# First batch's queries and keys loaded in rows of four tokens and turned by plain products; first chunk's input products in three single-pass products; a new table of costs and due times

## Chip, cores, metric

One core of one Trainium2 chip runs the kernel. The metric is device time in microseconds (us) of one execution; the time before is the median of 3 runs.

## What is computed

Three blocks in a row, in float32. The inputs are q, k, v of 4 batches x 8 heads x 576 tokens x 64 and, as 64-bit floats, the weights of two feed-forward blocks.

```python
# attention, per batch and head
q_d, k_d, v_d = (t.reshape(B, H, 144, 4, D).mean(axis=3) for t in (q, k, v))
out = repeat(softmax(q_d k_d^T / 8) v_d, 4) + softmax(where(|i-j| < 4, q k^T / 8, -1e9)) v
x = out as 2304 tokens x 512
# first block: 512 -> 2048 -> 512
h = x @ w_in;  g = where(h > 0, h, exp(min(h, 0)) - 1);  x2 = g @ w_out
# second block: 512 -> 2 x 1536 -> 512
y = (silu(x2 @ w_gate) * (x2 @ w_val)) @ w_o2
```

## The kernel before

**Stages.** The 2304 tokens of the first block are 8 chunks of 288 (`T1`), each made of 3 units of 96 tokens (`U`); a batch is 6 units. Chunk 0 is units 0 to 2 of batch 0, chunk 1 its units 3 to 5, chunk 2 the first half of batch 1. The head of the program does batch 0's attention. Then come 8 x 16 steps (chunk c, slice f of 128 of the 2048 inner columns): `gemm1` (h = w_in[f] x), the ELU (L984 and L992 on ACT, L988 on DVE), a split of g into two words (copy L307 or L309, subtraction L995 on POOL), and `gemm2`, which adds into 4 PSUM banks that hold the chunk's result. The attention of batches 1 to 3 and the preparation of later weights are threaded between these steps. The second block follows; it multiplies 2x2 blocks of matrices with 7 products (`add_seven`).

**Two ways to multiply.** A plain float32 product takes several passes in TensorE. `products` (L911 to L917) writes each operand as the sum of two words of type float32r, high and low, and makes three single-pass products: high x high (L915), high x low (L916), low x high (L917). A weight is split by `add_weight_split`: a copy gives the high word, a subtraction on POOL (L451) the low one. Chunk 0 uses plain products for both gemms (`add_whole`, L940 and L945), so its weights and its x need no split; chunks 1 to 7 use the three products for both.

**Weights.** They arrive as 64-bit floats (`load_w`, L363 and L368, 512 KB each) and are turned into float32 by `add_weights`: two ACT instructions (L404, L407) and two DVE instructions (L411, L413) per slice and matrix, 32 in the first block.

**Batch 0's attention.** `add_unit` loads q (96 tokens) and k (112) of one unit, token by partition, in pieces of 256 B (`load_rows`, L494), turns them with TensorE transpositions (L633), copies the result out of PSUM (`keep`, by L307 on ACT) and sums groups of four tokens (`add_sums`: L519 on DVE or L524 and L525 on POOL). `add_local` does the 7-wide local attention of a unit: scores (L541), mask (L558), maxima (L563), subtraction (L566), exp (L569), sum and reciprocal (L572 to L574), weighting (L577), 32x32 transposition (L580), spreading into `bd` (L309 or L307), values (L606). `add_pooled` does the pooled attention of two heads p: sums of four v rows (`add_rows`, L696 on DVE or L700 and L701 on POOL), scores (L717), maxima (L724, L725), exps (L730), weighting (L740 on DVE), transposition (L758), values (L774), and a copy to `xdT`. `add_split` adds local and pooled parts. For chunk 0 it is one DVE instruction per unit (L893, x<-f,xdT). For later chunks it adds (L893, f<-f,xdT, DVE or POOL), copies the high word (ACT or DVE) and subtracts for the low word (L903 on POOL).

**Order.** Every instruction group is a task of `Work`: the engine or engines that may run it with a cost, a due time, what it reads and writes. `Work.run` plays the tasks in a model and emits them engine by engine, the earliest due ready task first. Costs and due times (`START`, `STEP0`, `STEP`, `EAGER`, `URGENT`, `FREE`, `SLACK`, `spans`, `w2_away` and numbers in each `add`) decide the order; on the chip every engine then runs its own list in that order. DMAs are issued by SP in list order.

Of the kernel before, what the change touches and what calls it, by code (L numbers as in the profile page):

```python
# [27 lines left out]
KU = 112  # L28
# [109 lines left out]
class Work:  # L138
# [6 lines left out]
    CHANGE = 0.1  # L145
# [114 lines left out]
def attention_moe_moe(ctx: ExitStack, tc: tile.TileContext, q, k, v, w_in, w_out, w_gate, w_val, w_o2, ident_in, mask_in, band_in, picks_in, out):  # L260
# [20 lines left out]
    U0, U1 = 2, 19  # L281
# [95 lines left out]
    def add_words(due, raw, u, reads=()):  # L377
# [14 lines left out]
        add("act", 0.42, due - 4.1, rest, reads=[raw, *reads], writes=[raw])  # L392
        add("act", 0.42, due - 4, size, reads=[raw, *reads], writes=[u])
        return add("dve", 1.0, due - 2.5, words, reads=[raw, u], writes=[u])

    def add_weights(keys, dues, whole):

        made = {}
        for n, key in enumerate(keys):
# [16 lines left out]
            add("sp", 0.5, due - 36.0, lambda key=key, raw=raw: load_w(key, raw.t), writes=[raw], nbytes=P * 4096)  # L416
            add("act", 0.69, due - 4, rest, reads=[raw, w.whole], writes=[w])
            add("act", 0.69, due - 3.5, size, reads=[raw], writes=[ps])
            made[key] = add("dve", 1.5, due - 2.5, words, reads=[raw, w, ps], writes=[w, ps])
# [25 lines left out]
    def add_weight_split(key, due, w, copiers=COPIER):  # L445

        wt[key] = w
        u = ww[key]
        add(copiers, (0.62, 0.9)[:len(copiers)], due - 2, lambda engine="act": copy(engine, w.t[:, 0], u.t.bitcast(F32)),
            reads=[u], writes=[w], second=0)  # L450
        return add("pool", 1.3, due - 1, lambda: nc.gpsimd.tensor_tensor(  # L451
            out=w.t[:, 1], in0=u.t.bitcast(F32), in1=w.t[:, 0], op=ALU.subtract), reads=[u, w], writes=[w])
# [19 lines left out]
    PAD, QW = R - 1, U + QB - SB  # L472
    KW, LONG = KU + 2 * PAD + 2, S + 8
    turned = {
        name: pools["att"].tile(shape, F32, tag=name, name=name)
        for name, shape in (("qT", [P, NP * LONG]), ("kT", [P, NP * LONG]), ("bd", [P, 2, H, U]), ("sm", [P, 2, H, QB]))}
    places, longs = {}, {}
    for name, w in (("qT", QW), ("kT", KW)):
        places[name] = Places(lambda i, t=turned[name], w=w: t[:, i * NP * w:(i + 1) * NP * w].rearrange("p (a t) -> p a t", a=NP), LONG // w)
        longs[name] = Places(lambda i, t=turned[name]: t[:, i * LONG:(i + 1) * LONG], NP)  # L480
    for name in ("bd", "sm"):
        places[name] = Places(lambda i, t=turned[name]: t[:, i:i + 1], 2)
    twos = {name: Both(places[name], turned[name]) for name in ("bd", "sm")}
# [28 lines left out]
    def add_sums(due, x, to, reads, writes, cost):  # L512
# [3 lines left out]
        def pool(engine):  # L516
# [10 lines left out]
        return add(EITHER, cost, due, pool, reads=reads, writes=[*writes, half])  # L527

    def add_local(i, n, due, q_of, k_of, reads, off, tvs, then=()):

        start = i * U if n > 1 else 0
        sc, pvs = [att_bank(), att_bank()], [att_bank() for _ in range(n)]

        def scores():
            for u in range(n):
                for p in range(NP):
                    for s in range(NB):
                        a = start + u * U + s * SB
                        first = off + a - (R - 1)
                        for j in range(2):  # L540
                            nc.tensor.matmul(  # L541
                                sc[j].t[s * QB:(s + 1) * QB, (u * NP + p) * QB:(u * NP + p + 1) * QB],
                                q_of(p)[j * D:(j + 1) * D, a:a + QB], k_of(p)[j * D:(j + 1) * D, first:first + QB],
                                start=True, stop=True)

        sm, bd = (twos[name].new() if n > 1 else place(name) for name in ("sm", "bd"))
# [5 lines left out]
        add("pe", 0.8 * n, due + 2 - EAGER, scores, reads=reads, writes=[*sc, sm], slack=SLACK, kind="small", after=then)  # L552
# [12 lines left out]
        def less(engine):  # L565
            two(engine).tensor_tensor(out=both(sm.t), in0=both(sm.t), in1=sums_of().to_broadcast([P, n * H, QB]), op=ALU.subtract)  # L566
# [9 lines left out]
        def weight(engine):  # L576
# [13 lines left out]
        add("dve", cost(0.56, 0.28), due + 3 - FREE, masked, reads=sc, writes=[sm])  # L590
# [939 lines left out]
```

## Time and profile before

| | us |
|---|---|
| median of 3 runs (lowest, highest) | 963.61 (963.43, 965.06) |
| the profiled execution | 962.43 |
| its span, first to last instruction | 960.6 |
| busy in the span: PE / DVE / ACT / POOL | 924.7 / 587.9 / 519.6 / 488.8 |
| mean granted TensorE clock | 0.982 of full |

Three stretches of the span matter here: the head, until the first `gemm1` begins; chunk 0, in which both gemms are plain; and chunks 1 to 7. "Busy" is the union of an engine's instructions; an instruction's own duration can overlap the next by some hundredths of a microsecond. A plain product is recorded as two PE instructions, a float32r product as one.

### The profile page before, as it was taken

To read this page: it belongs to the slowest core of one execution; us is meant where nothing else is said; L and a number is where in the kernel's file an instruction comes from. 1 tells how busy PE (TensorE), PEld (TensorE's weight loads), DVE (VectorE), ACT (ScalarE), POOL (GpSimd) and SP (SyncE) were. 2 spreads that over 40 slices of the span, in tenths; PEclk is the share of its full clock that TensorE was granted. 3 is DMA by queue.
4 is the path that set the end of the run, shared out by engine and by line. 5 is a ranking of instruction groups with operands and counts; after the bars stand their busy time and mean duration, and the time that the engine had idled before them with its cause. 6 is when DMAs were issued, how large, how long until landed. Compare 5 with 4: busy or idle time off the path is not lost.

```text
span 960.6 us, 20374 instructions
## 1 busy us (share of the span) xinstructions
PE 924.7 (96%) x7738; PEld 838.2 (87%) x7738; DVE 587.9 (61%) x1023; ACT 519.6 (54%) x1191; POOL 488.8 (51%) x554
## 2 busy tenths in 40 slices
PE   6799999999989999999899999999999999999998
PEld 4577788899979999999899988888888887899998
DVE  5999777988886687646115567222222225886773
ACT  3878864665744665656445564634333426444441
POOL 5322994564553433428932537998777939100000
PEclk8689999999999999999999999999999999999999
DMA  9899514945673444546432254440313269953331
GB/s 173 251 319 250 93 40 121 164 144 141 162 159 94 129 135 124 154 128 199 149 94 81 83 184 182 162 176 23 121 51 114 99 208 322 314 165 112 124 129 44
DMA packets 189730, 142.07 MB, mean 148 GB/s; under 512 B 101184, under 2 KB 170944, under 8 KB 189632
## 3 DMA queue, kind: packets, MB, share of 16 engines
q1 hardware_dynamic: 189488, 140.50, 50.0%
q8 instruction: 61, 1.00, 0.4%
q14 instruction: 37, 0.30, 0.1%
q10 hardware_dynamic: 144, 0.26, 0.1%
HBM read 96.68 MB, written 44.04 MB: 146 GB/s over the span
## 4 chain that ended last, share of the span: by engine, by line
PE 85%; DVE 5%; ACT 2%; POOL 2%; SPq 2%; DMA 2%; issue 2%; DVEq 0%; ACTq 0%; POOLq 0%
PE bank L915 25%; PE bank L917 24%; PE bank L916 24%; PE bank L940 4%; PE bank L945 3%; PE bank L606 1%; PE bank L541 1%; SPq L662 1%; PE bank L817 1%; PE bank L823 1%; PE warm L1416 0%; DVE e L988 0%; PE bank L870 0%; DMA kT<-in_k_dram 0%; DMA x2d<-o 0%
## 5 line engine op out<-in xcount | busy, mean ns | idle before, releaser
L995 POOL TENSOR_TENSOR g<-e,g 128x288 fp32r<-128x288 f32 x112 | 96.3, 861 | 150.3 <-ACT g L307 115.6
L915 PE MATMUL bank<-x,w 128*128 128x288 f32 x448 | 136.3, 304 | 10.0 <-DVE e L988 9.8
L915 PE MATMUL bank<-g,w 128*128 128x288 f32 x448 | 135.2, 302 | 0.0
L916 PE MATMUL bank<-x,w 128*128 128x288 f32 x448 | 132.9, 297 | 1.6 <-POOL x L903 1.6
L915 PE MATMUL bank<-xs,wu 128*128 128x512 f32 x336 | 132.6, 395 | 0.5 <-DVE blk L1119 0.5
L916 PE MATMUL bank<-g,w 128*128 128x288 f32 x448 | 132.1, 295 | 0.7 <-issue 0.7
L916 PE MATMUL bank<-xs,wu 128*128 128x512 f32 x336 | 132.6, 395 | 0.0
L917 PE MATMUL bank<-xs,wu 128*128 128x512 f32 x336 | 132.6, 394 | 0.0
L917 PE MATMUL bank<-x,w 128*128 128x288 f32 x448 | 132.4, 296 | 0.0
L917 PE MATMUL bank<-g,w 128*128 128x288 f32 x448 | 131.8, 294 | 0.0
L1119 DVE TENSOR_TENSOR blk<-bank,blk 128x512 f32<-128x512 f32 x72 | 49.7, 691 | 99.1 <-PE bank L917 90.7
L915 PE MATMUL bank<-os,ys 128*128 128x256 f32 x378 | 107.3, 284 | 1.5 <-DVE o L1119 1.0
L917 PE MATMUL bank<-os,ys 128*128 128x256 f32 x378 | 107.0, 283 | 0.4 <-DVE ys L1087 0.4
L916 PE MATMUL bank<-os,ys 128*128 128x256 f32 x378 | 106.9, 283 | 0.0
L988 DVE SCALAR_TENSOR_TENSOR e<-e,bank 128x288 f32<-128x288 f32 x112 | 50.1, 449 | 82.9 <-ACT e L992 76.9
L915 PEld LDWEIGHTS bank<-x,w 128*128 128x128 f32 x448 | 84.6, 189 | 14.4 <-DVE e L988 13.1
L1116 ACT COPY blk<-bank 128x512 f32<-128x512 f32 x72 | 42.2, 586 | 88.6 <-PE bank L917 87.2
L984 ACT ACTIVATE e<-bank 128x288 f32<-128x288 f32 x112 | 45.7, 410 | 80.4 <-PE bank L917 50.8
L916 PEld LDWEIGHTS bank<-x,w 128*128 128x128 f32 x448 | 85.2, 190 | 1.9 <-POOL x L903 1.8
L915 PEld LDWEIGHTS bank<-g,w 128*128 128x128 f32 x448 | 84.0, 187 | 3.2 <-issue 1.5
L917 PEld LDWEIGHTS bank<-g,w 128*128 128x128 f32 x448 | 84.5, 189 | 0.8 <-issue 0.8
L917 PEld LDWEIGHTS bank<-x,w 128*128 128x128 f32 x448 | 85.1, 190 | 0.0
(170 smaller groups left out, 2315.2 us busy)
## 6 DMA issues: line engine op xcount, KB each, us to landing
yr<-yd SPq DMA_DIRECT2D x27, 512.0 KB
yd<-blk SPq DMA_DIRECT2D x24, 512.0 KB
os<-od SPq DMA_DIRECT2D x42, 256.0 KB
u<-wd SPq DMA_DIRECT2D x40, 256.0 KB
wd<-mid SPq DMA_DIRECT2D x72, 128.0 KB
w<-in_moe_w_in_dram SPq DMA_DIRECT2D x16, 512.0 KB
w<-in_moe_w_out_dram SPq DMA_DIRECT2D x16, 512.0 KB
w<-in_moe_w_out_dram SPq DMA_DIRECT2D x24, 256.0 KB
```

Of the source, the lines that this page charges most:

```text
L541: nc.tensor.matmul(sc[j].t[s * QB:(s + 1) * QB, (u * NP + p) * QB:(u * NP + p + 1) * QB], q_of(p)[j * D:(j + 1) * D, a:a + QB], k_of(p)[j ...
L606: nc.tensor.matmul(pvs[u].t[j * D:(j + 1) * D, p * U:(p + 1) * U], tvs[u].t[:, (2 * p + j) * D:(2 * p + j + 1) * D], bd.t[:, u, j * NP + p ...
L915: nc.tensor.matmul(ps, sh, mh, start=first, stop=False, skip_group_check=more)
L916: nc.tensor.matmul(ps, sh, ml, start=False, stop=False, skip_group_check=more)
L917: nc.tensor.matmul(ps, sl, mh, start=False, stop=last, skip_group_check=more)
L940: nc.tensor.matmul(h.t[:, :T1], wi.t[:, i * P:(i + 1) * P].bitcast(F32), x.t[:, i, 0].bitcast(F32), start=i == 0, stop=i == NP - 1)
L945: nc.tensor.matmul(acc[0][i].t[:, :T1], wo.t[:, i * P:(i + 1) * P].bitcast(F32), ge(), start=f == 0, stop=f == NF1 - 1)
L984: nc.scalar.activation(e.t, h.t[:, :T1], AF.Relu, scale=-1.0)
L988: nc.vector.scalar_tensor_tensor(out=e.t, in0=e.t, scalar=-1.0, op0=ALU.add, in1=h.t[:, :T1], op1=ALU.max)
L995: add("pool", 0.82, due - URGENT, lambda e=e, g=g: nc.gpsimd.tensor_tensor(out=g.t[:, 1], in0=e.t, in1=g.t[:, 0], op=ALU.subtract), reads= ...
L1116: return add("act", ps_copy, when(m) - 20, lambda: nc.scalar.copy(d(i), ps.t[:, :w]), reads=[ps], writes=of(i))
L1119: return add("dve", ps_sum, when(m) - 20, lambda: nc.vector.tensor_tensor(out=d(i), in0=ps.t[:, :w], in1=d(i), op=ALU.add), reads=[ps], wr ...
```

## The change

1. Batch 0's q and k come in 16 DMAs (`add_first_batch`), each 72 rows x 2 heads x 4 tokens, in pieces of 1 KB, instead of 12. Each is turned by 8 plain products with the identity (64 x 72 each) instead of 4 transpositions per load; a copy takes 288 columns out of PSUM, and the sums of four are made per piece of 72. Sums of k may only go to POOL now, those of q to DVE or POOL.
2. Sums of four v rows in batch 0 go to POOL alone (`VS`), its pooled weighting to DVE or POOL.
3. `gemm1` of chunk 0 makes the three float32r products. So the 16 input weights are split before chunk 0's steps, the copy by POOL or ACT (POOL preferred), and x of chunk 0 is split into two words as in later chunks.
4. New costs, due times, 19 instead of 17 slots for whole weights, and new rows for `sm` of batch 0.

Pairs of input weights now share a slot, as do pairs of output weights. The counts of the second block's instructions stay.

```diff
-    START, STEP0, STEP, STEP2 = 48.0, 4.1, 3.45, 7.9
+    START, STEP0, STEP, STEP2 = 29.4, 3.73, 3.68, 7.9
-    EAGER, URGENT, FREE, SLACK = 15.0, 14.0, 8.0, 1.0
+    VS, VC = EITHER[1:], (1.25,)
+    FIRST, VALUES, LATER, POOLED, EARLY, PREFER = -40.0, -16.0, 117.2, 1.5, 2.8, -16.0
+    EAGER, URGENT, FREE, SLACK = 32.9, 20.2, 14.9, 0.0
...
+    def add_first_batch(rows, ready):
+
+        sums[0] = sum_ring.new()
+        parts = {name: [longs[name].new(lambda p=p: [p]) for p in range(NP)] for name in ("qT", "kT")}
+        made = {}
+        for k, (p, u, which) in enumerate((p, u, which) for p in range(NP) for u in range(2) for which in range(2)):
+            name, start = (("qT", 0), ("kT", PAD))[which]
+            t, dst, pt = rows[k], parts[name][p], att_bank()
+            cols = slice(start + u * UPC * U, start + (u + 1) * UPC * U)
+            add("sp", 0.5, FIRST + 0.5 * k, lambda t=t, p=p, u=u, name=name: nc.sync.dma_start(
+                out=t.t, in_=rows_of(name[0], 0, u, 2 * p, 2 * p + 2)), writes=[t], nbytes=HALF * 2048 * 1.2)
+
+            def turn(t=t, pt=pt):
+                for r in range(R):
+                    for j in range(2):
+                        nc.tensor.matmul(
+                            pt.t[j * D:(j + 1) * D, :UPC * U].rearrange("c (g r) -> c g r", r=R)[:, :, r],
+                            t.t[:, j, r * D:(r + 1) * D], ident[:HALF, :HALF], start=True, stop=True)
+
+            add("pe", 0.62, FIRST + k - EAGER, turn, reads=[t], writes=[pt, dst], slack=SLACK, kind="small", after=ready[:1])
+            made[which, p, u] = add(COPIER, (0.41, 0.45), FIRST + k + 1, lambda engine, dst=dst, pt=pt, cols=cols: copy(
+                engine, dst.t[:, cols], pt.t[:, :UPC * U]), reads=[pt], writes=[dst], second=1)
+            summed.setdefault((0, p), []).append(add_sums(
...
+                holds=[dst], after=[made[which, p, u]], engines=EITHER[which:]))
+        return parts, made
...
-            add(EITHER, (1.0, 1.25), due, lambda engine, u=u, t=t: add_rows(u, t.t, engine), reads=[t], writes=[vs])
+            add(VS, VC, due, lambda engine="pool", u=u, t=t: add_rows(u, t.t, engine), reads=[t], writes=[vs])
...
-        if c == 0:
-            return add("dve", 0.8, due, lambda: both("dve", x.t[:, :, 0, cols].bitcast(F32)), reads=[xf, xdT[b]], writes=[x])
...
-        wi, wo, x = ww["in", f], ww["out", f], xt[0]
+        add_weight_split(("in", f), due - EARLY, w_slots.new(lambda: range(NW)), ("pool", "act"), PREFER)
+        wi, wo, x = wt["in", f], ww["out", f], xt[0]
...
         def gemm1():
             begun.append(1)
             for i in range(NP):
-                nc.tensor.matmul(
-                    h.t[:, :T1], wi.t[:, i * P:(i + 1) * P].bitcast(F32), x.t[:, i, 0].bitcast(F32), start=i == 0, stop=i == NP - 1)
+                cs = slice(i * P, (i + 1) * P)
+                products(h.t[:, :T1], (wi.t[:, 0, cs], wi.t[:, 1, cs]), (x.t[:, i, 0], x.t[:, i, 1]), i == 0, i == NP - 1)
...
-            return time1(2 * NF1) + (time1(6.9 * NF1) - time1(2 * NF1)) * m / (2 * len(w2))
+            return time1(2.4 * NF1) + (time1(7.6 * NF1) - time1(2.4 * NF1)) * m / (2 * len(w2))
...
-        spans = {1: (18, 25), 2: (40, 50), 3: (70, 80)}
+        spans = {1: (14.8, 16.8), 2: (28.1, 79.7), 3: (66.3, 178.5)}
```

What moves, at three places. The names are tiles: `bank` a PSUM bank, `w` a slot that holds weights or, in the head, attention rows, `x` the chunk's input, `g` the ELU's output.

PE, end of the head, before:

```order
L758 MATMUL bank<-ident,w 72x72 x8
L541 MATMUL bank<-kT,qT 32x32 x32
L774 MATMUL bank<-prT,vs 64x144 x4
L606 MATMUL bank<-bd,w 64x96 x8
L940 MATMUL bank<-x,w 128x288 x8
L945 MATMUL bank<-g,w 128x288 x4
```

PE, end of the head, now:

```order
L605 MATMUL bank<-bd,w 64x96 x8
L748 MATMUL bank<-ident,w 72x72 x8
L764 MATMUL bank<-w,vs 64x144 x4
L605 MATMUL bank<-bd,w 64x96 x8
L538 MATMUL bank<-kT,qT 32x32 x32
L903 MATMUL bank<-x,w 128x288
L904 MATMUL bank<-x,w 128x288
L905 MATMUL bank<-x,w 128x288
```

The first slices of `gemm1` are single-pass products now; three slices of them (36 products) stand ahead of the first `gemm2`, where two slices (8 plain products) did.

POOL, at the end of the head, before:

```order
L577 TENSOR_TENSOR sm<-sm,st 128x256
L566 TENSOR_TENSOR sm<-sm,st 128x256
L451 TENSOR_TENSOR w<-w 128x512 x2
L893 TENSOR_TENSOR f<-f,xdT 128x384
L577 TENSOR_TENSOR sm<-sm,st 128x256
```

POOL, at the end of the head, now (the last row is the last one that the first `gemm1` waits for):

```order
L506 MEMSET w 32x512
L310 CAST w<-w 128x512
L452 TENSOR_TENSOR w<-w 128x512
L883 TENSOR_TENSOR f<-f,xdT 128x384
L452 TENSOR_TENSOR w<-w 128x512
L891 TENSOR_TENSOR x<-f,x 128x4x96 x2
L452 TENSOR_TENSOR w<-w 128x512
L891 TENSOR_TENSOR x<-f,x 128x4x96
```

Splits of three input weights and of x stand on POOL ahead of the first `gemm1`; before, nothing on POOL did after the last weighting L577.

POOL, in chunk 6, where the second block's weights are combined (`s`, `t`, `u`, `wu`) between the subtractions of g; before:

```order
L995 TENSOR_TENSOR g_6441<-e_6373,g_6441 128x288
L1087 TENSOR_TENSOR wu_6357<-u_6304,wu_6357 128x256
L1087 TENSOR_TENSOR wu_6357<-s_6305,wu_6357 128x256 x2
L1087 TENSOR_TENSOR t_6478<-u_6331 128x256 x2
L1087 TENSOR_TENSOR t_6478<-u_6331,t_6478 128x256
L1087 TENSOR_TENSOR wu_6357<-s_6305,wu_6357 128x256
L1087 TENSOR_TENSOR t_6478<-u_6331,t_6478 128x256
L1087 TENSOR_TENSOR s_6355<-u_6354 128x256 x2
L1087 TENSOR_TENSOR s_6355<-s_6355,u_6354 128x256
L995 TENSOR_TENSOR g_6538<-e_6421,g_6538 128x288
```

The same work now:

```order
L983 TENSOR_TENSOR g_6790<-e_6760,g_6790 128x288
L1075 TENSOR_TENSOR s_6699<-u_6698,s_6699 128x256
L1075 TENSOR_TENSOR wu_6765<-u_6698,wu_6765 128x256 x2
L1075 TENSOR_TENSOR wu_6765<-s_6699,wu_6765 128x256
L983 TENSOR_TENSOR g_6831<-e_6807,g_6831 128x288
L1075 TENSOR_TENSOR wu_6765<-u_6698,wu_6765 128x256
L1075 TENSOR_TENSOR s_6723<-u_6722 128x256
L1075 TENSOR_TENSOR wu_6765<-s_6699,wu_6765 128x256 x3
L983 TENSOR_TENSOR g_6896<-e_6851,g_6896 128x288
L1075 TENSOR_TENSOR oh_6918<-u_6717,oh_6880 128x256
```

Before, 11 combinations stood between two subtractions of g; now no more than 5 do here.

## Rows read from the trace of the kernel before

**Rows 1.** Page, part 1: busy us (share of the span), instructions.

```profile
PE 924.7 (96%) x7738; PEld 838.2 (87%) x7738; DVE 587.9 (61%) x1023; ACT 519.6 (54%) x1191; POOL 488.8 (51%) x554
```

**Rows 2.** Chain that ended last: start us, us, what.

```profile
46.06 3.12 DVE x L893 x3
...
49.22 6.71 PE bank L940 x16
...
112.27 0.13 PE bank L915
...
113.86 1.94 PE bank L945 x8
```

**Rows 3.** Stretches: us, busy us of PE, PEld, DVE, ACT, POOL, granted clock, DMA.

```profile
9.50:49.20 39.70, 29.30 (x588) 23.47 (x588) 35.69 (x94) 28.65 (x85) 18.57 (x39) 0.68 0.96 227
...
49.20:112.30 63.10, 63.08 (x274) 48.78 (x275) 54.67 (x93) 53.66 (x112) 26.25 (x30) 0.96 0.93 249
112.30:518.00 405.70, 390.43 (x4198) 372.86 (x4197) 271.41 (x516) 234.25 (x594) 216.90 (x252) 1.00 0.49 132
...
260.00:280.00 20.00, 16.09 (x131) 15.10 (x130) 17.79 (x29) 10.90 (x29) 12.96 (x15) 0.91 0.75 152
440.00:480.00 40.00, 36.34 (x270) 35.64 (x270) 13.25 (x25) 22.95 (x63) 36.60 (x48) 1.00 0.54 180
```

**Rows 4.** Groups of DVE, 9.5 to 49.2: count, busy us, mean ns of one.

```profile
L696 DVE TENSOR_REDUCE vs<-w 72x128 f32<-72x512 f32 x4 | 4.1, 1021 | 0.0
L740 DVE TENSOR_TENSOR w<-w,su 72x576 f32<-72x576 f32 x4 | 2.9, 745 | 0.0
L563 DVE TENSOR_REDUCE st<-sm 128x8 f32<-128x256 f32 x6 | 2.4, 400 | 0.0
```

**Rows 5.** Groups of DVE, 0 to 560.

```profile
L413 DVE SCALAR_TENSOR_TENSOR w<-w,bank 128x512 int32<-128x512 int32 x32 | 22.0, 688 | 1.1
L893 DVE TENSOR_TENSOR f<-f,xdT 128x384 f32<-128x384 f32 x13 | 9.5, 757 | 1.9 <-ACT xdT L307 1.1 <-ACT f L307 0.8
L309 DVE CAST x<-f 128x384 fp32r<-128x384 f32 x11 | 9.2, 854 | 0.9 <-PE bank L917 0.9
```

**Rows 6.** Groups of POOL, 0 to 560.

```profile
L451 POOL TENSOR_TENSOR w<-w 128x512 fp32r<-128x512 f32 x32 | 41.3, 1317 | 11.5 <-ACT w L307 11.5
L903 POOL TENSOR_TENSOR x<-f,x 128x384 fp32r<-128x384 f32 x21 | 22.2, 1070 | 10.8 <-ACT bank L404 8.6 <-ACT x L307 1.9 <-DVE x L309 0.3
L800 POOL TENSOR_TENSOR praw<-praw 72x256 f32<-72x256 f32 x19 | 14.7, 775 | 18.4 <-DMA praw<-in_v_dram 18.4
L856 POOL TENSOR_TENSOR pr<-pr,su 72x576 f32<-72x576 f32 x11 | 12.9, 1176 | 19.9 <-DVE su L853 12.6 <-ACT mid L380 7.3
L801 POOL TENSOR_TENSOR vs<-praw 72x128 f32<-72x128 f32 x19 | 9.2, 486 | 6.2 <-PE bank L817 5.1
L525 POOL TENSOR_TENSOR sums<-half 128x96 f32<-128x96 f32 x6 | 2.1, 357 | 0.5
L524 POOL TENSOR_TENSOR half<-kT 128x192 f32<-128x192 f32 x4 | 2.1, 513 | 8.9 <-ACT kT L307 8.8
```

**Rows 7.** Timeline of PE in the head: start us, us, what.

```profile
31.63 0.69 PE L758 MATMUL bank<-ident,w 72*72 72x72 f32 x8
...
42.06 1.18 PE L758 MATMUL bank<-ident,w 72*72 72x72 f32 x8
```

**Rows 8.** Timeline of DVE: two of its instructions in chunks 1 and 3.

```profile
143.54 3.30 DVE L566 TENSOR_TENSOR sm<-sm,st 128x512 f32<-128x512 f32 x1
...
264.37 4.11 DVE L309 CAST x<-f 128x384 fp32r<-128x384 f32 x1
```

**Rows 9.** Timeline of POOL beside them.

```profile
143.77 2.53 POOL L451 TENSOR_TENSOR w<-w 128x512 fp32r<-128x512 f32 x2
...
267.27 0.99 POOL L903 TENSOR_TENSOR x<-f,x 128x384 fp32r<-128x384 f32 x1
```

**Rows 10.** Waits of PE: us in total, times, longest us.

```profile
PE bank L915 <- DVE e L988: 9.8, 8, 3.9
```

More of the change, by code (lines that the diff above doesn't have):

```diff
@@ L27 @@
 U = NB * SB
-KU = 112
 CR = 64
@@ L144 @@
     SECOND = 65.0
-    CHANGE = 0.1
+    CHANGE = 0.15
     FIXED = 2.0
@@ L414, in words @@
                     out=t, in0=raw.t[:, :, 1], scalar=-0x80000000, op0=ALU.bitwise_and, in1=p, op1=ALU.bitwise_or)
[L416 to L419, printed above, removed]
+            add("sp", 0.5, due - 46.8, lambda key=key, raw=raw: load_w(key, raw.t), writes=[raw], nbytes=P * 4096)
+            add("act", 0.67, due - 4, rest, reads=[raw, w.whole], writes=[w])
+            add("act", 0.64, due - 3.5, size, reads=[raw], writes=[ps])
+            made[key] = add("dve", 1.4, due - 2.5, words, reads=[raw, w, ps], writes=[w, ps])
             ww[key] = w
@@ L510, in load_values, with add_sums, pool @@
                 load_rows("v", b, a, min(hi - a, QB // 2 if hi - lo < QB else QB), t, p0 + a - lo)
-    def add_sums(due, x, to, reads, writes, cost):
+    def add_sums(due, x, to, reads, writes, cost, engines=EITHER, **kw):
         half = half_ring.new()
-        def pool(engine):
+        def pool(engine=engines[0]):
             src, dst = x(), to()
@@ L525, in pool, with add_local @@
                 nc.gpsimd.tensor_tensor(out=dst, in0=h[(*cut, 0)], in1=h[(*cut, 1)], op=ALU.add)
-        return add(EITHER, cost, due, pool, reads=reads, writes=[*writes, half])
-    def add_local(i, n, due, q_of, k_of, reads, off, tvs, then=()):
-        start = i * U if n > 1 else 0
+        return add(engines, cost, due, pool, reads=reads, writes=[*writes, half], **kw)
+    def add_local(i, n, due, parts, made, tvs, masks=(), then=(), sm=None):
         sc, pvs = [att_bank(), att_bank()], [att_bank() for _ in range(n)]
@@ L550, in add_local @@
         sums_of = lambda: st.t[:, :n * H]
-        add("pe", 0.8 * n, due + 2 - EAGER, scores, reads=reads, writes=[*sc, sm], slack=SLACK, kind="small", after=then)
+        add("pe", 0.8 * n, due + 2 - EAGER, scores, holds=[x for name in parts for x in parts[name]], writes=[*sc, sm],
+            slack=SLACK, kind="small", after=[*made, *then])
         edges = [0 if k == 0 else 2 if k == NU - 1 else 1 for k in range(i, i + n)]
@@ L599, in add_local @@
         else:
-            add("act", 2.1, due + 6, lambda: spread("act"), reads=[sm], writes=[bd])
+            add("act", 2.05, due + 6, lambda: spread("act"), reads=[sm], writes=[bd])
         def values(us):
@@ L689, in add_pooled @@
         vs = vs_ring.new()
-        mx, nm, su, prT = (small[n].new() for n in ("mx", "nm", "su", "prT"))
-        pr = pr or small["pr"].new()
+        mx, nm, su = (small[n].new() for n in ("mx", "nm", "su"))
         qk = sums[b]
@@ L746, in add_pooled @@
         add("dve", 0.4, due + 4, norm, reads=[su], writes=[su])
[L747 to L750 removed]
+        add(EITHER, (0.78, 1.15), due + 4.3, weight, reads=[pr, su], writes=[pr])
         pws = [att_bank(), att_bank()]
@@ L1001, in gemm2 @@
                     products(acc[c][i].t[:, :T1], (wo.t[:, 0, cs], wo.t[:, 1, cs]), (g.t[:, 0], g.t[:, 1]), f == 0, f == NF1 - 1)
-            last[c] = [add("pe", 12 * 0.134, due + STEP, gemm2, reads=[wo, g], writes=acc[c], after=last.get(c, ()), slack=1.0)]
+            last[c] = [add("pe", 12 * 0.1325, due + STEP, gemm2, reads=[wo, g], writes=acc[c], after=last.get(c, ()), slack=1.0)]
             if f == NF1 - 1:
@@ L1401, in parts @@
             return [Part(buf, buf.t[:, a].bitcast(F32)) for a in range(n)]
-        rows = [parts(2) for _ in range(NU)]
+        rows = [x for _ in range(2 * NP) for x in parts(2)]
         vals = [x for _ in range(NU // 2) for x in parts(2)]
```

155 lines of the change are left out of this document (65 added, 90 removed).

## Prediction

> **What bounds the kernel now.** The first view is the busy time by engine [rows 1]: PE has 924.7 of 960.6 us, every other engine 61% or less. So time can only go in two ways: fewer PE cycles, or fewer of the 35.9 us in which PE stands. The second view, the chain that ended last [rows 2], says where the stages lie. The first `gemm1` begins at 49.22, right behind three DVE additions of 3.12 us that make chunk 0's x; the head ends there. At 112.27 the first float32r product of chunk 1 starts, so chunk 0 took 63.05 us. The third view, the stretches [rows 3], gives the limit of each. In the head DVE is busy 35.69 of 39.70 us and PE mostly waits for it. In chunk 0 PE is busy 63.08 of 63.10 us: every PE cycle taken out there is time, as long as DVE (54.67) and ACT (53.66) keep up. From 112.3 to 518 PE stands for 405.70 - 390.43 = 15.3 us; nearly 10 of the waits in the first block's products end on the ELU's DVE step [rows 10]. The second block's instructions keep their counts, and I cost it at nothing: PE is its cover, and the change gives PE no other work there.
>
> **The sum** is made against the profiled execution, 962.43 us; the median of the runs shown, 963.61, is 1.2 above it.
>
> *Head.* Two engines must get their lists done before the first `gemm1`. DVE has 35.69 us of work now [rows 3]. It loses four v sums (4.1) and two of four weightings (2 x 0.745), and, since units 3 to 5 come later, five of eleven local reductions (5 x 0.40) [rows 4], and the three additions into x (3.1) [rows 2]. It gains one pair of weight-word instructions (2 x 0.688), two additions (2 x 0.757) and a cast of x (0.854) [rows 5]. The six sums of four it had become seven shorter ones; I set these equal. That is -10.7 + 3.7 = -7.0, so 28.7 us. With the 4.0 us that DVE idles now it needs 32.7 from about 9.5, when the first sums start: 42.2. POOL had 18.57 us in this stretch [rows 3] and becomes as heavy: nine pairs of sums at 0.513 + 0.357 or less (they are shorter now), eight v pairs at 0.775 + 0.486, two weightings at 1.176, three low words of weights at 1.317 and a cast with no row of its own, which I put at the same 1.3, one addition and three local steps (2.9 together, an estimate from the additions' 0.757 on DVE and the 72x256 row's 0.775), and three low words of x at 1.070 [rows 6]: 7.8 + 10.1 + 2.4 + 5.3 + 2.9 + 3.2 = 31.7, from about 10.5 to 42.2. Two engines that each reach 42, each waiting for the other now and then, and a last step of x on POOL behind a cast: I take 44.5, **-4.7**. Ends: 41.5 if both run dense (-7.7); 49.2 (0) if the turning decides. Its price has no row: 16 groups of 8 small products. The nearest, 8 transpositions of 72x72, take 0.69 us at the high clock and 1.18 at the low one [rows 7], so 11 to 19 us of PE from about 7.5. At 11 it hides behind the loads and the first pooled heads; at 19 it ends at 26.5 and the cover is gone. PE works without a gap while it turns, so I stay near 11.
>
> *Chunk 0's products.* A slice of `gemm1` in the three products takes 113.86 - 112.27 = 1.59 us, and a plain slice 1.94, the row shown being `gemm2`'s, of the same shape [rows 2]. 16 x 0.35 = **-5.6**. The first slices run at half clock now (6.71 us for two) and I leave that as it is: 12 single-pass products cost double there too.
>
> *Chunk 0's stalls.* The stage shrinks from 63.1 to 57.5 us. If DVE kept 54.67 and ACT 53.66 us of work [rows 3], they would be 95% and 93% full, with bursts at the start, where three input splits, a cast by POOL or ACT and 1.3 us of POOL each now stand ahead of each slice. PE had no wait here; I give **+2**. Ends: 0, because three slices of `gemm1` are ahead of the first `gemm2`, and 5.6, which is all that the products saved.
>
> *Chunks 1 to 7.* Of the 15.3 us two pieces are known. In 440 to 480 PE stands 3.7 us while POOL is busy 36.60 of 40 [rows 3]: eleven combinations stand between two subtractions of g. They now come in groups of five or fewer, so the wait of g goes, and nothing else is late there (DVE has 13.25 of 40). In 260 to 280 PE stands 3.9 us and then runs at a granted clock of 0.91 on average [rows 3], part of the stretch at 1.2 instead of 2.4 GHz, about 1.5 us. There one DVE cast took 4.11 us [rows 8] in the middle of batch 2's clump of attention. `spans` now spreads batch 2 over steps 28 to 80 instead of 40 to 50, and the 16 input splits are no longer POOL's in chunk 1. Together 9.1. The small rest I leave, and give one new stall: **-8**. Ends: 0, a new clump for every one that goes, and -13.
>
> Sum: -4.7 - 5.6 + 2 - 8 = -16.3, so 946.1 for the profiled execution, and with the 1.2 us **947 us** for the median.
>
> **A rule against it.** POOL gets more work and DVE meets it. The rows show DVE instructions that stretch until POOL pauses: L566 from 143.54 to 146.84 while POOL ran two weight splits until 146.30, and the cast from 264.37 to 268.48 while POOL's last step of a series ended at 268.26 [rows 8, 9]. The Trainium skill, "SBUF — State Buffer", section "Who interferes with whom", states that DVE with two SBUF inputs, or in a two-port mode, and GpSimd share a port pair, and that the second to issue is blocked for the whole instruction. By that rule one such step waits for one POOL instruction, at most 1.3 us here; the trace shows it held over several in a row. By the rule, eight such DVE steps in the head at half of 1.3 would add 5.2 us, and the sum would be 952; I keep the rows' way, where most steps are not held, and make the worst of it a rival.
>
> **Rivals.**
> - *Both dense* (faster still): the head ends at 41.5 and the new order leaves 13 us less of standing, chunk 0 without a stall. -7.7 - 5.6 - 13 = -26.3: 937. For it: due times that spread every clump. Against: POOL's list alone reaches 42.
> - *Chunk 0 goes to DVE and ACT.* Words of weights, ELU and late local attention fill them, the saved products show as waits of `gemm1`, and of the later gain half is left: -4.7 - 5.6 + 5.6 - 4 = -8.7: 955. For it: 95% and 93%. Against: DVE and ACT keep ahead of PE by many slices now.
> - *POOL's series hold DVE* (slower than before): in the head and in chunk 0 POOL's rows stand back to back for the first time, and the DVE step in the chain (weighting, addition, cast) waits for the end of a series as in rows 8, at 3.3 to 4.1 us each, mean 3.7. To be slower than now it must eat 16.3 + 1.9 us, so it decides from five holds in the chain; six give 947 + 22 = 969. For it: two such holds already, at a POOL load of half. Against: in the head POOL's own rows wait for DVE, which gives pauses.
> - *The products save nothing.* If three products per slice took as long as a plain one, 5.6 us would be missing: 953. The chunk 1 rows, same shape and operands, exclude it but for the clock at the start.
>
> **Numbers.** 0.2%, 1.9 us, is about what a measurement of this kernel can tell from no change. Forecast 0.60 (941 to 953, the unsaved products in it), both dense 0.14, chunk 0 on DVE and ACT 0.20, held DVE 0.05, and 0.01 for an even end between them. Faster 0.93, same 0.02, slower 0.05. The range reaches to 936 and 958: below, the dense case; above, a head that gains 0 (4.7 more) and a chunk 0 that gives all back (3.6 more), with part of the later gain gone.
>
> **What would show it.** Right: the first `gemm1` begins at 43 to 46, behind POOL's low word of x; chunk 0 lasts 58 to 61 us; POOL is busy over 80% of the head; PE stands about 7 us from chunk 1 to the end of the first block; no wait in 440 to 480. Wrong: a first `gemm1` at 48 or later, PE waits on DVE or ACT of more than 4 us in chunk 0, or as many waits on the ELU as now in chunks 1 to 7.

## The result, and the profile after

The change takes **947.64 us** (median; 947.18 to 948.56), beside 964.34 for the kernel before on the same chip: ratio 0.9828 (95% interval 0.9811 to 0.9845). 947 was forecast. But the sum is right and its terms are not: one has the wrong sign, another is half of what was measured. One of the four executions of the run weights_held took 1435.04 us; its median below is that of the other three.

The table goes by three marks of the profiled executions: where the first product of chunk 0 begins, where chunk 1's first product begins, and the end of the span.

| stretch | before | after | difference | forecast |
|---|---|---|---|---|
| head, to the first product of chunk 0 | 49.2 | 52.9 | +3.7 | -4.7 |
| chunk 0, to chunk 1's first product | 63.1 | 60.8 | -2.3 | -3.6 |
| from there to the end | 848.3 | 831.8 | -16.5 | -8 |
| span | 960.6 | 945.5 | -15.1 | -16.3 |

The page, part 1, answers to [rows 1]: PE's busy time fell by 6.8 us, its standing time from 35.9 to 27.6.

```profile
PE 917.9 (97%) x8010; PEld 840.5 (89%) x8010; DVE 577.8 (61%) x1014; ACT 515.3 (54%) x1185; POOL 511.3 (54%) x586
```

The stretches of after, with the columns of [rows 3]:

```profile
9.50:52.90 43.40, 29.80 (x737) 24.38 (x737) 31.49 (x78) 27.49 (x85) 28.44 (x52) 0.67 0.85 232
52.90:113.70 60.80, 58.35 (x361) 50.74 (x361) 57.37 (x104) 54.48 (x115) 45.73 (x54) 0.96 0.90 231
113.70:518.00 404.30, 401.28 (x4305) 386.04 (x4304) 274.88 (x524) 243.54 (x615) 218.18 (x260) 1.00 0.50 135
260.00:280.00 20.00, 20.00 (x270) 19.79 (x269) 13.69 (x27) 11.28 (x27) 5.95 (x8) 1.00 0.77 146
440.00:480.00 40.00, 39.58 (x297) 39.08 (x296) 19.34 (x30) 26.14 (x72) 35.49 (x45) 1.00 0.57 182
```

In the head DVE has less work than before (31.49 against 35.69 us) and still ends later: it stands 11.9 us instead of 4.0. In chunk 0 PE now stands 2.45 us. From chunk 1 to 518 it stands 3.0 us instead of 15.3, and both stretches that the prediction picked out are mended: 260 to 280 is full at full clock, and 440 to 480 lost 0.4 us instead of 3.7, though POOL is as full there as it was. The wait for the ELU's DVE step, 9.8 us in [rows 10], is almost gone in the waits of PE (us in total, times, longest):

```profile
PE bank L903 <- DVE e L976: 0.4, 1, 0.4
```

The chain of after through the head (start us, us, what) answers to [rows 2]:

```profile
18.30 0.74 PE bank L538 x50
19.05 2.36 issue
21.41 1.51 PE bank L538 x79
22.93 0.69 PE bank L710 x4
23.61 2.72 issue
26.34 1.72 PE bank L710 x12
...
46.85 0.69 DVE w L414
47.54 0.21 DVE w L556
47.76 0.66 ACT bank L405
48.41 0.54 ACT w L306
...
49.02 1.27 POOL w L452
50.30 2.23 POOL x L891 x2
52.53 1.36 POOL w L452
53.88 0.97 POOL x L891
...
54.90 0.61 PE bank L904
```

Two things are new. PE stands twice, 5.1 us together, for nothing that the profile shows ("issue"). And behind DVE's last step on this chain (it ends at 47.75) come 7 us of ACT and POOL in series, the splits of weights and x, before the second product can start at 54.90. The prediction ends the head there, behind POOL's low word of x; the table's mark, the first product, needs only the high words. DVE's timeline, 20 to 30, shows who waited for PE: 2.20 and 3.60 of DVE's 11.9 us (in brackets: idle before, and its releaser).

```profile
22.29 0.49 DVE L556 TENSOR_TENSOR w<-bank,mask 128x128 f32<-128x128 f32 x2 [2.20 <-PE bank L538]
...
27.12 0.82 DVE L717 TENSOR_REDUCE mx<-bank 72x2 f32<-72x288 f32 x2 [3.60 <-PE bank L710]
```

### The profile page after: what moved, and what is told of

The parts are those of the page before. It is cut to its first block, busy times and chain, and to the rows that moved or that the text cites. A ratio compares the mean times of both kernels' runs of the same rounds, so it can differ in the third digit from the quotient of the medians.

```text
span 945.5 us, 20979 instructions
## 1 busy us (share of the span) xinstructions
PE 917.9 (97%) x8010; PEld 840.5 (89%) x8010; DVE 577.8 (61%) x1014; ACT 515.3 (54%) x1185; POOL 511.3 (54%) x586
## 4 chain that ended last, share of the span: by engine, by line
PE 90%; DVE 4%; issue 2%; DMA 1%; ACT 1%; POOL 1%; DVEq 0%; SPq 0%; ACTq 0%; POOLq 0%
PE bank L903 27%; PE bank L905 26%; PE bank L904 26%; PE bank L934 3%; PE bank L538 2%; PE bank L605 1%; DMA w<-in_moe_w_val_dram 1%; PE bank L807 1%; PE bank L813 1%; PE bank L630 1%; PE bank L860 1%; PE warm L1409 1%; DMA x2d<-o 0%; DVE mid L388 0%; POOL x L891 0%
## 5 line engine op out<-in xcount | busy, mean ns | idle before, releaser
L903 PE MATMUL bank<-x,w 128*128 128x288 f32 x512 | 157.9, 308 | 4.9 <-ACT w L408 3.5
L904 PE MATMUL bank<-x,w 128*128 128x288 f32 x512 | 151.8, 297 | 1.4 <-POOL x L891 1.4
L905 PE MATMUL bank<-x,w 128*128 128x288 f32 x512 | 151.3, 295 | 0.0
L903 PEld LDWEIGHTS bank<-x,w 128*128 128x128 f32 x512 | 96.8, 189 | 9.4 <-POOL x L891 3.6
L904 PEld LDWEIGHTS bank<-x,w 128*128 128x128 f32 x512 | 97.4, 190 | 2.6 <-POOL x L891 2.0
L905 PEld LDWEIGHTS bank<-x,w 128*128 128x128 f32 x512 | 97.3, 190 | 0.0
```

Source lines behind the costliest of these rows:

```text
L903: nc.tensor.matmul(ps, sh, mh, start=first, stop=False, skip_group_check=more)
L904: nc.tensor.matmul(ps, sh, ml, start=False, stop=False, skip_group_check=more)
L905: nc.tensor.matmul(ps, sl, mh, start=False, stop=last, skip_group_check=more)
```

## Experiments

All medians are set against the same kernel before, 964 to 965 us in each comparison. The last columns are marks of each profiled execution; the first block's last steps can lie behind the mark of the second block.

| run | median us | first product | chunk 0's last gemm2 ends | second block's first product | span | PE stands between the last two marks |
|---|---|---|---|---|---|---|
| before | 964.3 | 49.2 | 120.2 | 536.3 | 960.6 | 15.3 |
| the change | 947.6 | 52.9 | 121.0 | 527.7 | 945.5 | 3.0 |
| before_late_dues | 955.9 | 50.3 | 121.6 | 534.9 | 954.2 | 7.8 |
| late_dues_before | 954.8 | 51.7 | 121.1 | 533.8 | 952.7 | 8.0 |
| plain_first_chunk | 959.5 | 50.3 | 119.7 | 538.3 | 957.2 | 9.5 |
| old_head | 962.8 | 51.0 | 123.0 | 535.8 | 960.1 | 11.7 |
| old_head_same_order | 952.9 | 51.2 | 123.5 | 533.3 | 950.9 | 5.7 |
| plain_same_order | 959.7 | 50.1 | 120.7 | 535.2 | 952.5 | 7.5 |
| old_head_plain_same_order | 965.2 | 49.3 | 123.6 | 545.9 | 963.3 | 12.4 |
| start_plus_2 | 958.3 | 49.5 | 119.0 | 538.0 | 956.8 | 10.3 |
| start_minus_2 | 962.2 | 54.0 | 121.8 | 527.5 | 961.6 | 11.9 |
| weights_held | 946.7 | 50.1 | 120.0 | 527.5 | 944.9 | 3.9 |
| weights_late | 950.9 | 54.0 | 127.7 | 535.4 | 952.8 | 2.9 |
| mask_first | 951.7 | 56.9 | 126.8 | 532.8 | 950.3 | 2.4 |

**1. The later due times alone, each way.** The kernel before with the new due times of batches 1 to 3 (`EAGER1` and `FREE1` are `EAGER` and `FREE` for them, and `STEP` is 3.68 as in the change):

```diff
-        spans = {1: (18, 25), 2: (40, 50), 3: (70, 80)}
+        spans = {1: (14.8, 16.8), 2: (28.1, 79.7), 3: (66.3, 178.5)}
...
-            add_pooled_all(b, lo + 4, lo - 10, 3.0)
+            add_pooled_all(b, lo + 9.0, lo - 2.1, 6.9)
```

> The kernel before, with only the due times of batches 1 to 3 (their loads, turning, windows, blocks, input splits and the second layer's weights) taken from the change; head, plain first products and costs stay. Theory A, the gain behind chunk 0 (16.6 us) is the later batches' order: 949 to 954 us, TensorE idle in 112 to 530 under 6 us (15.3 before). Rival B, it is POOL and VectorE relieved in chunk 0, because the input weights are split earlier: 960 to 965 us and an idle time like before's.

Measured: 955.85, ratio 0.9911 (0.9887 to 0.9934). PE stands 7.8 us. The mirror of it, the changed kernel with the old numbers (the same lines the other way round; `STEP` stays at 3.68):

> The changed kernel, with the due times of batches 1 to 3 put back to those of before; its first 70 TensorE steps are the changed kernel's. Theory A: the later gain goes, 958 to 963 us, with waits behind VectorE's and POOL's series in chunks 2 to 7. Rival B: 947 to 951 us.

Measured: 954.75, ratio 0.9903 (0.9879 to 0.9927); PE stands 8.0 us. Both fall between the theories: the due times are worth 7 to 9 us, about half of what was gained behind chunk 0.

**2. The parts of the head, one undone at a time.** First the products of chunk 0 (which weights share a slot is again as before, too):

```diff
-        add_weight_split(("in", f), due - EARLY, w_slots.new(lambda: range(NW)), ("pool", "act"), PREFER)
-        wi, wo, x = wt["in", f], ww["out", f], xt[0]
+        wi, wo, x = ww["in", f], ww["out", f], xt[0]
...
+        add_weight_split(("in", f), time1(NF1 + f), w_slots.new(split_places), COPIER[:1])
```

> The changed kernel with chunk 0's input products plain again: x and the input weights are not split ahead of them, the weights' splits go back to chunk 1. Theory C, the three products save 16 x 0.35 us, but the splits that they need at the head's end (weights and x on POOL) cost the head 3 to 5 us: 947 to 951 us, first product at 48 to 50 us. Rival D, the splits cost the head nothing: 952 to 955 us, first product still at 52 to 53 us.

Measured: 959.52, ratio 0.9949 (0.9931 to 0.9967). The first product comes at 50.3, as theory C has it, but the loss is 12 us, more than either allows, and lies behind chunk 0: that stage ends at 119.7, 1.3 us ahead of the change's, so up to there the products bring nothing, their saving being paid for in the head. What is lost comes from PE's waits (120 to 560) and from PE's granted clock, which is at half, 1.2 GHz, from 138 to 142 and from 155 to 159:

```profile
PE bank L905 <- DVE e L978: 4.9, 6, 1.3
PE bank L860 <- DVE f L308: 2.7, 1, 2.7
PE bank L807 <- DVE prT L308: 1.6, 1, 1.6
```

Then the head, with `add_unit` and its loads in the place of the new functions:

```diff
-        parts, made = add_first_batch(rows, ready)
...
+            xfs[n] = add_unit(n, 4.0 * n, -40 + 2 * n, rows=(*rows[n], vals[n]), late=0.0 if n < UPC else 24.0,
```

> The changed kernel with the head of the kernel before (whole-row loads, turned by transposition, one unit after the other); products, later due times and costs stay. Theory E, the new head itself is the loss (TensorE stood 5.1 us with no releaser in 19 to 27 us): 942 to 945 us, first product at 47 to 50 us. Rival F, the splits at the head's end are the loss and come with the old head too: 946 to 950 us, first product at 52 to 54 us. Rival G, the new head gains what was forecast and something else hides it: 951 us or more.

Measured: 962.77, ratio 0.9982 (0.9971 to 0.9993): nearly all of the gain is gone, though the first product comes 1.9 us earlier than with the change. So Rival G's number came out, and the head was not the place. PE's waits of this run (120 to 560):

```profile
PE bank L914 <- DVE e L987: 9.4, 10, 2.3
```

Most of it lies in 440 to 480, where PE is busy 33.26 of 40 us. The waits of that stretch go back to POOL: PE waits for DVE's step on e, DVE for ACT's, and ACT for the subtraction of g, which still reads an e (440 to 482; us in total, times, longest):

```profile
ACT e L983 <- POOL g L994: 9.5, 7, 2.1
```

POOL's timeline tells why. There it makes the second block's weights, and between these steps the subtraction of g, once per slice. A slice takes PE 2 x 1.59 = 3.2 us [rows 2]. POOL is busy 19.92 of 20 us from 460 to 480 here and all 20 in the change. In this run six subtractions begin within 20.83 us, five distances of 4.17 on average:

```profile
460.07 0.81 POOL L994 TENSOR_TENSOR g<-e,g 128x288 fp32r<-128x288 f32 x1
...
480.90 0.81 POOL L994 TENSOR_TENSOR g<-e,g 128x288 fp32r<-128x288 f32 x1
```

In the changed kernel seven begin within 18.52 us, six distances of 3.09, just under the slice's time:

```profile
460.89 0.81 POOL L983 TENSOR_TENSOR g<-e,g 128x288 fp32r<-128x288 f32 x1
...
479.41 0.81 POOL L983 TENSOR_TENSOR g<-e,g 128x288 fp32r<-128x288 f32 x1
```

What differs is the order that the planner made. The later due times and costs do not stay, although the expectation says so: the run also has `START` 48.0 as before (29.4 in the change), before's 17 slots for whole weights, its loads of the first weights (36.0 ahead of their due time instead of 46.8) and before's costs of many later steps, among them 0.82 instead of 0.86 for the subtraction of g. Whether the head or these numbers drew the other order was not tested. Either way "undo one part" was no clean experiment: the edit also drew a new order for 850 us.

**3. The same order, forced.** In the next runs each engine's order from early chunk 1 on is the changed kernel's own: the planner is given that list, and may start a listed step on an engine only when it is next.

```diff
+            if t.id in LATE and ORDER[engine][self.trail.get(engine, 0):][:1] != [t.id]:
+                continue
```

> The kernel of the run old_head (the head of before, everything else as in the change), with each engine's order from the start of chunk 1 on forced to be the changed kernel's own, step by step, so that the planner can't answer the other head with another order. Theory H, what is gained behind chunk 0 is that order and nothing else: 947 to 952 us, TensorE idle in chunks 1 to 7 near 3 us (11.7 in old_head), first product still at 50 to 52 us. Rival I, the old head holds the later chunks up physically (buffers, transfers that come late): 957 to 961 us and an idle time of 8 us or more.

Measured: 952.92, ratio 0.9864 (0.9835 to 0.9894). Theory H, a little over its range, with PE's idle time (5.7 us) between the two theories: 9.8 of the 15.1 us that old_head lost were the order. Then the plain products, with the new head and with the old:

> The kernel of the run plain_first_chunk (new head, chunk 0's input products plain, the weights' splits in chunk 1), with the order from early chunk 1 on forced to be the changed kernel's. Theory P, that run's 959.5 us came mostly from another order, and the products themselves are worth 16 x 0.35 us less the 2.6 us that their splits cost the head and 2.5 us of waits in chunk 0: 948 to 952 us. Rival Q, the splits that go back to chunk 1 hold POOL and VectorE there whatever the order: 955 to 960 us, with 4 us or more of TensorE's waits in 120 to 200.

Measured: 959.67, ratio 0.9952 (0.9927 to 0.9977); the runs scatter from 954.3 to 966.4, and the profiled one is near the lower end (span 952.5). Rival Q, with that scatter: PE stands 5.4 us in 120 to 200, first for the pooled attention of batch 1. The 32 steps of the input splits stand in no forced list, so the planner puts them between the listed ones. The waits say:

```profile
PE bank L922 <- ACT prT L421: 2.9, 1, 2.9
```

The three products bring nothing up to the end of chunk 0 here either (120.7 without them, 121.0 with). The 7.0 us that the profiled execution loses come behind it: PE stands 4.5 us more, and from 126.3 to 133.2 its granted clock is at half, which makes 6.5 us of work out of 3.2.

> Old head and plain first products, with the order from early chunk 1 on forced to be the changed kernel's: what the order alone makes of the kernel before. Theory R, parts add up (old head +5.3 as with the products): 5 us above the run plain_same_order, 953 to 957 us. Rival S, the new head is worth something only with the products, whose splits the old head delays: within 2 us of plain_same_order.

Measured: 965.21, ratio 1.0004 (0.9993 to 1.0014). Theory R in its difference (5.5 us over plain_same_order), not in its number. So, under one order for chunks 1 to 7:

| | three products | plain |
|---|---|---|
| new head | 947.6 | 959.7 |
| old head | 952.9 | 965.2 |

The head is worth 5.3 to 5.5 us in either column, the products 12 in either row, as far as the scattered run allows: its interval is 2.4 us to either side, and by the profiled executions the upper row gives 7.0 and the plain column 10.8. Within that the parts add up once the order is held. The order alone, on the program before, gives nothing (965.2 for 964.3); it fits the program that it was made for. In that run PE stands 4.9 and 4.4 us in chunk 1, and its clock is at half from 127 to 138 and from 148 to 155. Two limits go with the table. Most of the products' 12 us is what this order costs a program that it was not made for: with the old head, plain products and an order of its own, before_late_dues took 955.9, 9.3 us less than under this order and only 3.0 more than old_head_same_order. And the old head keeps before's later loads of the first weights, which alone cost the new head 3.3 us (weights_late, below).

**4. One number of the planner moved.**

```diff
-    START, STEP0, STEP, STEP2 = 29.4, 3.73, 3.68, 7.9
+    START, STEP0, STEP, STEP2 = 31.4, 3.73, 3.68, 7.9
```

> The changed kernel with one number of the planner moved by 2 us: START 31.4 instead of 29.4 (due times of all chunks; nothing computed changes). Theory T, the table of numbers fits this one program, and any shift gives another order with waits of its own in chunks 2 to 7: 950 to 958 us. Rival U, the order is robust: 946 to 949 us.

Measured: 958.31, ratio 0.9933 (0.9913 to 0.9953).

> The same with START 27.4. Theory T: 950 to 958 us. Rival U: 946 to 949 us.

Measured: 962.22, ratio 0.9974 (0.996 to 0.9988): theory T, and at the second even past its range. 2 us of a due time, with nothing computed otherwise, cost 11 and 15 us. PE stands 7.3 and 8.9 us longer than in the change between the last two marks. The rest is mostly the granted clock. In the first run it is at half from 275.6 to 282.4, where PE had stood 3.0 us (until 276.1); in the second from 191.2 to 201.4 and from 283.3 to 290.1, where PE had stood 5.9 (until 195.1) and 2.9 us (until 282.5). PE is busy 6.3 and 13.1 us in these stretches, and half of that is the price, 3.1 and 6.5 us; the change has no such stretch behind chunk 0. The waits of PE in the two runs (58 to 560) have nothing in common but the kind:

```profile
PE bank L903 <- DVE e L976: 4.6, 10, 0.9
PE bank L860 <- POOL pr L846: 3.0, 1, 3.0
```

```profile
PE bank L860 <- DVE pr L846: 5.9, 1, 5.9
PE bank L860 <- POOL pr L846: 2.9, 1, 2.9
```

**5. The head's lost time** (later order forced in all three). PE's timeline of the changed kernel shows at which instructions it stood:

```profile
18.23 0.81 PE L538 MATMUL bank<-kT,qT 64*32 64x32 f32 x68
21.41 1.51 PE L538 MATMUL bank<-kT,qT 64*32 64x32 f32 x124 [2.36 <-issue]
22.86 0.76 PE L710 MATMUL bank<-sums 64*72 64x144 f32 x4
26.34 1.72 PE L710 MATMUL bank<-sums 64*72 64x144 f32 x12 [2.72 <-issue]
```

Between the two lie 124 + 4 = 128 products, with their weight loads 256 instructions. Page part 3 of after has a queue for instructions (packets, MB, share):

```profile
q8 instruction: 63, 1.03, 0.5%
```

63 packets for PE's 8010 products and 8010 weight loads are one packet per 254 instructions (before: 61 for 2 x 7738, the same 254). So the theory was that PE waits for its own instructions, behind data on the same engines: in 17 to 26 they carried the first weights and the first values.

```diff
-            add("sp", 0.5, due - 46.8, lambda key=key, raw=raw: load_w(key, raw.t), writes=[raw], nbytes=P * 4096)
+            add("sp", 0.5, due - 46.8, lambda key=key, raw=raw: load_w(key, raw.t), writes=[raw], nbytes=P * 4096, after=scored)
```

> The changed kernel, in which the loads of the first layer's weights wait until TensorE has done the windows' first scores, and the order from chunk 1 on is forced to be the changed kernel's. Theory J, TensorE's 5.1 us with no releaser in 19 to 27 us are its own instructions, fetched behind the data of the weights: these stalls fall under 2 us, and the first products come 2 to 3.5 us earlier: 944 to 946 us. Rival K, the transfers have no part in it: the stalls stay at 4 us or more, 947 to 949 us. Rival L, the stalls go, but VectorE's list sets the end of the head: 946 to 948 us, first products within 1 us of the changed kernel's.

Measured: 946.67, ratio 0.9815 (0.9795 to 0.9836): no difference from the change that can be measured. The first stand all but went, the second stayed, at the same products:

```profile
18.40 0.81 PE L655 MATMUL bank<-kT,qT 64*32 64x32 f32 x68
19.38 1.30 PE L655 MATMUL bank<-kT,qT 64*32 64x32 f32 x124 [0.17 <-issue]
20.75 0.57 PE L827 MATMUL bank<-sums 64*72 64x144 f32 x4
23.44 1.27 PE L827 MATMUL bank<-sums 64*72 64x144 f32 x12 [2.12 <-issue]
```

The first product came 2.8 us earlier, as theory J has it, and the total stayed, as its rivals have it. The 2.8 us were given back on the way: the second product waited 2.3 us for POOL's low word of x (1.4 in the change), chunk 0 waited 1.0 for ACT's ELU, its end came 1.1 us earlier and the second block 0.2.

> The changed kernel, in which the first layer's weights are loaded behind the blocks' first values instead of ahead of them, without a wait, and the order from early chunk 1 on forced to be the changed kernel's. Theory J, narrowed: any data in flight delays TensorE's instructions; with the values' transfers in the place of the weights' the engine still stands at the same two instructions (after 68 of the first window scores, and 128 matmuls further on), for 3 to 6 us together, and the first products come within 1.5 us of the changed kernel's: 946 to 949 us. Rival V, only the weights' large transfers do it: together under 2.5 us, first products 2 us or more earlier, 944 to 947 us.

In this run the edit is 36.0 for 46.8 in the same line, without the wait. Measured: 950.90, ratio 0.9859 (0.9838 to 0.9881). The stands are there again, at the same products, 4.0 us together:

```profile
21.23 1.51 PE L655 MATMUL bank<-kT,qT 64*32 64x32 f32 x124 [2.09 <-issue]
22.67 0.76 PE L827 MATMUL bank<-sums 64*72 64x144 f32 x4
25.34 1.72 PE L827 MATMUL bank<-sums 64*72 64x144 f32 x12 [1.91 <-issue]
```

Theory J, narrowed, holds for the stands. The times of the instruction queue's packets in the traces say what ends them. All are of 16,384 bytes; in the change two are in transfer from 18.70 to 19.94 and from 23.34 to 24.84, and PE goes on at 21.41 and 26.34, 1.5 us behind the end of each:

| run | PE goes on at | packet in transfer | PE behind its end |
|---|---|---|---|
| the change | 21.41, 26.34 | 18.70 to 19.94, 23.34 to 24.84 | 1.5, 1.5 |
| weights_held | 19.38, 23.44 | 16.98 to 18.13, 20.53 to 22.03 | 1.2, 1.4 |
| weights_late | 21.23, 25.34 | 18.62 to 19.79, 22.40 to 23.89 | 1.4, 1.5 |
| late_dues_before | 19.63, 25.93 | 17.28 to 18.24, 23.25 to 24.50 | 1.4, 1.4 |

The same holds in all kept traces: of the 33 stands of PE over 0.3 us that the profile puts down to nothing, 32 end 1.2 to 1.6 us behind such a packet, all 20 in the heads among them (the other is at 113.3 in old_head_plain_same_order). The total of weights_late is above both ranges, because the weights now came too late: the first product waited 4.6 us for ACT's step on weight words, and chunk 0 waited 4.3 us for DVE's.

```diff
-        ready = [add("sp", 0.5, FIRST + 0.9, load_ident, nbytes=P * 512), add("sp", 2.0, FIRST + 4.6, load_mask, nbytes=P * 128)]
+        ready = [add("sp", 0.5, FIRST + 0.9, load_ident, nbytes=P * 512), add("sp", 2.0, FIRST - 1.0, load_mask, nbytes=P * 128)]
```

> The changed kernel, with the mask loaded ahead of the queries and keys instead of behind ten of their loads, and the order from chunk 1 on forced to be the changed kernel's. Theory M, POOL's sums of keys, which stood behind the mask's copies until 12.7 us, are what makes the head late: sums from 9 us on, first products 2 to 3 us earlier, 944 to 946 us. Rival N, the sums' late start is made up before the head's end: 947 to 949 us, first products within 1 us of the changed kernel's.

Measured: 951.65, ratio 0.9866 (0.9844 to 0.9888): slower, against both theories. POOL's sums did begin at 10.13 instead of 12.69. But the planner answered with another head, all turning ahead of the first pooled scores; PE stood in the middle of the turning and went on at half clock (granted 0.50 from 16.8 to 64.5, in the change only from 20.8 to 44.7 and from 48.1 to 58.3), the turning ended 2.4 us later, and the first product came at 56.9. PE's timeline there:

```profile
9.74 5.83 PE L747 MATMUL bank<-ident,w 72*64 72x72 f32 x158 [0.84 <-ACT qT L423]
17.30 3.38 PE L747 MATMUL bank<-ident,w 72*64 72x72 f32 x50 [1.74 <-issue]
```

With 12 warming products and 48 + 158 turning ones the stand comes about 218 products in; the two of the changed kernel come at 12 + 256 + 8 + 68 = 344 and at 472. The steps are 126 and 128 (some records can be missing). mask_first stands three more times, at 344, 471 and 596. No run here beat the change by more than the measurement can tell.

## Why the prediction was right and wrong

- **Head, -4.7 forecast, +3.7 measured: wrong sign.** The step that failed is "with the 4.0 us that DVE idles now it needs 32.7 from about 9.5". DVE's list came to 31.5 us instead of 28.7, and it idled 11.9. 5.8 us of that were waits for PE in its two stands, which end as PE's own instructions arrive, a stall that the sum put at nothing and that the trace of before does not show in its head. Holding the weights back won 2.8 us of it for the first product. In the list itself eight DVE steps were held by POOL, 4.7 us in all (see Rivals), a term that the prediction named and also put at nothing. The other step is the tail: 2.3 us were allowed behind the lists' end at 42.2, and the splits of weights and x, ACT and POOL in series, took 7 from DVE's last step to the second product. POOL was 28.44 us busy, near the 31.7 forecast, but in a longer head: 66%, not 80. The turning was priced rightly (the 16 groups ended at 18.3) and did not decide.
- **What the head is worth** still is 5.3 us, under one order and with its earlier loads of the weights (952.9 to 947.6); that it is near the 4.7 forecast is luck, since it does not lie at the place. Of the 5.4 us in the spans the first product gives -1.7, chunk 0 (to its last gemm2) 4.1 and chunks 1 to 7 with the rest 3.0. With the old head chunk 0 stands 4.0 us instead of 2.45 and PE is at half clock until 62.0, with the change until 58.3 (granted 0.60 over 50 to 65, after the change 0.72). Of the last 3.0 us 2.7 are PE's longer waits, most for the ELU's DVE step; why they come under the same order was not taken apart.
- **Chunk 0's products, -5.6, and stalls, +2.** Together -3.6 was forecast and -2.3 measured. PE stands 2.45 us there, 1.4 for x at the second product and 1.0 for the ELU. PE's work fell by 4.7 us although 1.3 us of attention moved in (48 local value products for 32, and 8 of batch 1's pooled scores), so the products saved about 6.0. Inside the stage the mechanism held and the stall was near its size; the moved 1.3 us were left out. But the saving is paid for in the head: with plain products, all else and the order held, the first product comes 2.8 us earlier and chunk 0 ends at the same time (120.7 for 121.0). What was missed is where the products' worth lies: behind chunk 0, as the input splits leave chunk 1, where they stand in the way of batch 1's attention. (In the chain of plain_same_order from 112 to 150 POOL's splits of weights take 22%.) Under the forced order that is 7 to 12 us, with an order made for plain products about 3 (before_late_dues against old_head_same_order). The prediction named it ("the 16 input splits are no longer POOL's in chunk 1") and gave it no price of its own.
- **Chunks 1 to 7, -8 forecast, -16.5 measured to the end of the span.** The mechanism was right at both places named. Mis-sized is "the small rest I leave, and give one new stall": all of the -16.5 lies in the first block (behind its last gemm2 both kernels take 405.9 us), and of 15.3 us of standing only 3.0 are left (-12.3), the low clock is gone (3.3 us of work at half clock, so 1.7), and no new stall came. Of the 2.5 us that remain 0.6 are batch 1's first pooled scores, which now lie ahead of the mark; the rest was not taken apart. The ends, 0 to -13, were those of an order not yet known to fit; START moved by 2 us shows that the price of a misfit is as large as this whole term.
- **Rivals.** Chunk 0 on DVE and ACT did not come (1.0 us of waits, DVE 57.37 of 60.8). POOL's series did not hold DVE at 3.3 to 4.1 us a step, the longest hold in the head being 0.9 us. But single POOL instructions did hold it: eight DVE steps of the head began while one ran, ended 0.0 to 0.4 us behind its end and took 0.3 to 0.9 us longer than the shortest of their kinds, 4.7 us together, 2.8 us of it in the five ahead of 47.75. Four of the eight, whose shortest take 0.11, 0.39, 0.54 and 0.54 (timeline of DVE):

```profile
31.45 0.72 DVE L729 TENSOR_SCALAR su<-su 72x4 f32<-72x4 f32 x1
...
37.17 1.32 DVE L564 TENSOR_TENSOR w<-w,st 128x256 f32<-128x256 f32 x1
...
47.85 1.24 DVE L883 TENSOR_TENSOR f<-f,xdT 128x384 f32<-128x384 f32 x1
...
50.34 1.33 DVE L883 TENSOR_TENSOR f<-f,xdT 128x384 f32<-128x384 f32 x1
```

  Beside the second POOL's weighting ran from 37.06 to 38.20. Not every step that met POOL was held: one of the second's kind took 0.39 us at 32.30, while POOL's step beside it took 0.78 instead of 0.45. The eight agree with the Trainium skill, "SBUF — State Buffer", section "Who interferes with whom", by which the second to issue waits for the whole instruction of the other. The rule's term for the head, eight such steps and 5.2 us, came out nearly as it stood (eight and 4.7), and the head was late; its total of 952 did not come, because the later chunks gave 8.5 us more than the sum had.

The total was right by luck: a head that was forecast 8.4 us too good and later chunks that were forecast 8.5 too bad cancelled.

## What to carry to other kernels

Where a planner emits the order, an edit of one part draws a new order for all the rest: here 2 us in one due time cost 11 to 15 us, and undoing a part cost 12 to 15, of which up to two thirds were the order. Read PE's granted clock beside its waits: in start_minus_2 it cost 6.5 us on top of the waits. Hold the later order fixed before a part is judged, and search the table anew after each edit. And price the serial tail behind a list (here ACT and POOL, 7 us) apart from the list.

## What was not expected of the hardware

PE stood at fixed places of its instruction stream, 125 to 128 products with their weight loads apart (218, 344, 471 or 472, 596), for nothing that the profile names; its instructions come in packets of 254 on average. Nine runs with the new head show such stands in it, at one or more of these places and 0.17 to 4.61 us long; the three runs with the old head and the new products or order have one of 3.3 to 3.5 us at product 468, the kernel before none in its head. That it waits for its own instructions is what the packets' times show: it goes on 1.2 to 1.6 us behind the end of one. What sets the length is then how early the transfer begins: 2.2 us before PE ran out in the stand of 0.17, 0.3 before in that of 2.72, 1.9 after in that of 4.61. Why it begins late stays open: with the weights held back one stand went and the other did not, and with the values in the weights' place both were there. During the first stand of the change, at 20.8, the granted clock fell to half; it was 0.54 on average in 20 to 30, 1.00 from 9.5 to 19.
